# DeltaNet and top-2 experts on one core: the experts' part in a written order, and four early tiles instead of five

## The chip, the cores and the metric

One Trainium2 chip, one core. The metric is the device time of one execution in microseconds (us). The engines are named PE (TensorE), ACT (ScalarE), DVE (VectorE), POOL (GpSimd) and SP (SyncE, which here only issues DMAs). All data is fp32.

## The reference

A delta-rule attention over 4 batches, 8 heads, 768 steps and 48 columns a head; its output, as 3072 tokens of 384 columns, goes through a noisy top-2 router with 8 experts, each two matrices of 384 × 1024 and 1024 × 384 with a ReLU between.

```python
# attention, for each step t
y[:, :, t] = einsum('bhd,bhde->bhe', q[:, :, t], state)
v_old = einsum('bhde,bhd->bhe', state, kt)
state = state + bt * einsum('bhd,bhe->bhde', kt, vt - v_old)
# experts; x is y as (3072, 384)
noisy = x @ w_gate + log1p(exp(x @ w_noise)) * noise
# the two largest per token, their softmax is top2_w
for e in range(8):
    for k in range(2):
        mask = top2[:, k] == e
        out[mask] += top2_w[mask, k, None] * (relu(x[mask] @ w1[e]) @ w2[e])
```

## The kernel before

**Attention.** `deltanet()` computes attention in six steps of 128 positions (512 tokens each) and routes in four rounds: steps 0 and 1, 2 and 3, 4, 5. Every piece of it is a job for one engine, with a cost, what it reads and writes, and for some a due time; a planner (`Jobs`) writes out the order of all engines from these, and the program keeps to that order. As soon as a round is routed, each row of it (384 columns and four numbers: token, gates, expert) is spread by indirect DMAs (`spread`, L385) into `rows_x` in HBM, expert by expert: 3072 places for each expert, of which the first ones fill.

**Early tiles.** So that PE has work while the last steps are routed and spread, the first rows of expert 0 are computed inside this stage, in buffers that attention no longer needs (`early`, L1200). The table `EARLY` (L22) says which tiles of 128 rows: four tiles with tokens up to step 3 and a fifth one with tokens up to step 4. `cut` (L1165) moves the count of rows on, where fewer have come so far, so that these tiles hold only rows of the tokens so far. For a set of tiles, SP loads rows, PE transposes them (L1258), PE multiplies with `w1e` (L1284), ACT does the ReLU (L1294), PE multiplies with `w2e` (L1307), DVE multiplies with the gate (`early_gate`) on the way out of PSUM (L1321), and POOL scatters into `out_dram`, adding nothing yet (L426).

**Experts.** What follows is ordered by the scheduler of the framework, from the order in which the code stands and from its own estimates, so an instruction may pass others of its engine.

- `rest()` (L1666) does the remaining rows of expert 0 up to 832, here 192. SP loads them into `xq` (32 partitions, L1545) and their numbers into `m` (L1556); `places` (L1573) makes the index and the gate of each row on DVE (L1579, L401, L405); DVE turns `xq` into `xe_r` by 32 × 32 transposes (L1680); PE multiplies with `w1e` (L1688), ACT does the ReLU, PE multiplies with `w2e` (L1696 for the whole tile, L1701 for the last 64 rows); DVE multiplies with the gate (L1705 to L1707), POOL scatters. Between these, DVE makes the 21 sums of blocks of expert 1's `w1` (`add_up` with `SUMS_W`, L1502), POOL zeroes both `sums` (L1484) and makes the four sums of blocks of its `w2` (`t_w`, L1509), and the rows of expert 1 are loaded, turned into `xe` (L1588, six turns) and summed into `s_x` (`SUMS_X`, L1502, twelve sums).
- Experts 1 to 7 then have the same form, each with 832 rows. `first()` (L1593) computes the hidden layer by a fast block scheme: a table `PLAN` of 40 half products (two passes each, matmul at L1536 into one of five banks `inner`), with additions into `hT` on DVE (L1613), copies and ReLUs on ACT (L1619, L1608) and, on DVE, the sums of the hidden layer `s_h` (L1524), four for each half. `second()` (L1621) is a 2 × 2 scheme with seven products for each of three pairs of tiles; each product is followed by one or two additions into `sums` by DVE, times the gate (`add_gated`, L1438), and the steps share the banks `outer` and three of `inner`. The two first pairs go step by step together (`both`), then the third with the last 64 rows (`last_rows`, L1651).
- In the code, the preparation of the next expert stands in between: SP's loads at the start; the sums of `w1` on POOL and the next index and gate behind the hidden sums; two turns after each of three steps; all twelve row sums ahead of the third pair; after the last scatter (`put`) the sums of `w2` on POOL and the gathers (L417) that fetch what is in `out_dram` for the next expert's tokens into the other `sums`.
- At the end `values_load` reads the largest count of rows on all engines; only if an expert had more than 832 rows, a slow branch does the rest. It does not run here.

Of the kernel before, what the change touches and what calls it, by code (L numbers as in the profile page):

```python
# [9 lines left out]
FP32 = mybir.dt.float32  # L10
# [8 lines left out]
Q = 32  # L19
TILES = 6  # L20
MORE = 64
EARLY = {3: (0, 4), 4: (4, 5)}  # L22
# [207 lines left out]
def kernel(  # L230
# [201 lines left out]
    def deltanet(ictx):  # L432
# [754 lines left out]
        early_index, early_gate = sb([128, 5], "early_index", I32), sb([128, 5], "early_gate")  # L1187
# [12 lines left out]
        def early(s):  # L1200
# [12 lines left out]
            if lo == 0:  # L1213
                xr = old_k[0:4]
                xe = [*old_kT[0:2], old_q[0]]
                hT = old_k
                xr = [(x[:, 0:ROW], key) for x, key in xr]
                hT = [(x[:, 0:rows], key) for x, key in hT]
            else:
                (x, key), (y, key_y), *z = old_kT[2:6]  # L1220
                xr = [(x[:, 0:ROW], key)]
                xe = [(y[:, do * 128 : (do + 1) * 128], key_y) for do in range(KT)]
                hT = [
                    (z[fo // 4][0][:, fo % 4 * 128 : (fo % 4 + 1) * 128], z[fo // 4][1])
                    for fo in range(FT)
                ]
# [72 lines left out]
            for i in range(n):  # L1299
# [3 lines left out]
                for f0 in range(0, FT, 2):  # L1303
# [16 lines left out]
                    DVE, 0.6,  # L1320
                    lambda got=got, p=p, at=at: nc.vector.tensor_scalar_mul(  # L1321
# [125 lines left out]
    with ExitStack() as ectx:  # L1447
# [9 lines left out]
        bank_x = outer[0:2]  # L1457
# [13 lines left out]
        nc.tensor.matmul(bank_x[0][:, 0:E], ones, before)  # L1471
        nc.vector.tensor_copy(counts, bank_x[0][:, 0:E])
        nc.vector.tensor_reduce(out=most, in_=counts, axis=AX.X, op=ALU.max)
        nc.vector.tensor_copy(most_i, most)


# [6 lines left out]
        for got in sums:  # L1483
            nc.gpsimd.memset(got, 0.0)  # L1484

# [14 lines left out]
        def add_up(engine, sums, block):  # L1500
            for to, x, y, sign in sums:
                engine.tensor_tensor(  # L1502
                    out=block(to), in0=block(x), in1=block(y),
                    op=ALU.add if sign == "+" else ALU.subtract,
                )

# [159 lines left out]
        def rest():  # L1666

            w1e, w2e = w_even_tiles
            t0 = EARLY[4][1]
            rows = slice(t0 * 128, ROWS)  # L1670
            cols = rows.stop - rows.start
            got = sums[0]
            load_rows(
                0, rows.start,
                [(128, 0, rows.start, ROWS - MORE), (MORE, TILES - t0, ROWS - MORE, ROWS)],
            )
            index, gate = places(0, TILES - t0, TILES - t0)
            xe_r = moe.tile([128, KT, cols], FP32, name="xe_r")
            for b in range(KT):
                nc.vector.transpose(  # L1680
                    out=xe_r[:, b], in_=xq[:, rows.start // Q :, b:QD:KT]
                )
            load_rows(1)
            banks = [*inner, outer[2]]
            for fo in range(FT):
                p_h = banks[fo % 6][:, 0:cols]
# [5 lines left out]
                nc.scalar.activation(hT[:, fo, 0:cols], p_h, ACTF.Relu)  # L1692
            add_up(nc.vector, SUMS_W, blocks[0])
            p_o, p_m = bank_x[0][:, 0:DM], bank_x[1][:, 0:DM]
            for fo in range(FT):
                nc.tensor.matmul(  # L1696
                    p_o, hT[:, fo, 0:128], w2e[:, fo], start=(fo == 0), stop=(fo == FT - 1)
                )
            halves = [slice(lo, lo + MORE) for lo in (0, 64)]
            for fo in range(FT):  # L1700
                nc.tensor.matmul(  # L1701
                    p_m[halves[fo % 2]], hT[:, fo, 128:cols], w2e[:, fo],
# [185 lines left out]
```

## Time and profile before

| | |
|---|---|
| median of 3 runs | 863.03 us (862.18 to 864.03) |
| profiled execution | 860.22 us |
| its span, first to last instruction | 858.1 us |
| mean granted clock of PE over the span | 0.896 of full speed |
| experts 1 to 7, start of the first product (us) | 424.27, 487.11, 550.35, 610.00, 669.66, 729.35, 788.72 |
| end of PE's last pass | 847.39 us |

Times in the trace count from the first instruction. A row of the timeline is a group of equal instructions that follow each other: its start, the time from the start of the first to the end of the last, engine, line, operation, output and inputs, shapes and count. In brackets stands the idle time ahead of it on its engine and what ended that. Instructions of an engine overlap a little, so n of them take less than n times the duration of one. A matmul of fp32 data is recorded as two passes.

### The profile page before, as it was taken

How to read it: one execution, taken by the hardware profiler on the slowest of the kernel's cores; microseconds unless marked ns; L12 is line 12 of the kernel's file. 1: busy time of each engine (PE TensorE's matmuls, PEld its weight loads, DVE VectorE, ACT ScalarE, POOL GpSimd, SP SyncE). 2: the span in 40 equal slices, each digit the busy share in tenths (PEclk: the TensorE clock that was granted, in tenths of full speed). 3: DMA queues.
4: the chain of work that ended last, by engine and by line, in shares of the span. 5: the costliest groups of instructions: out<-in, count | busy, mean ns of one | idle time of the engine just before them, and what ended most of it. 6: DMA issues, size and time to landing. Idle time of an engine off the chain costs nothing.

```text
span 858.1 us, 21611 instructions
## 1 busy us (share of the span) xinstructions
PE 749.2 (87%) x8957; PEld 576.1 (67%) x8957; DVE 591.0 (69%) x1347; ACT 310.4 (36%) x733; POOL 389.8 (45%) x424
## 2 busy tenths in 40 slices
PE   4756879887898898993899999999999999999995
PEld 3546668776697785562548748759668678587594
DVE  5996899989978653007479589388487595694651
ACT  3573558755734543110152141150240330520510
POOL 3021312121552745116275774576684785776311
PEclk8566959895769799996999999999999999999998
DMA  4789733724522323601664626317325425401201
GB/s 65 135 231 258 154 95 99 196 55 131 132 80 58 118 88 125 208 25 36 141 164 108 156 59 144 121 56 167 123 96 103 140 82 99 145 0 58 58 25 37
DMA packets 141724, 93.74 MB, mean 109 GB/s; under 512 B 115242, under 2 KB 134089, under 8 KB 140592
## 3 DMA queue, kind: packets, MB, share of 16 engines
q1 hardware_dynamic: 129952, 64.54, 31.3%
q0 software_dynamic: 9552, 27.33, 9.5%
q8 instruction: 72, 1.18, 0.5%
q10 hardware_dynamic: 2112, 0.39, 0.3%
q14 instruction: 36, 0.29, 0.1%
HBM read 58.82 MB, written 34.81 MB: 109 GB/s over the span
## 4 chain that ended last, share of the span: by engine, by line
PE 52%; DVE 14%; issue 3%; ACT 1%; POOL 0%; DVEq 0%; POOLq 0%; ACTq 0%
PE inner L1536 22%; PE outer L1536 11%; DVE s_x L1502 4%; PE pair L1284 3%; PE pair L1307 3%; PE inner L1659 2%; DVE sums L1438 2%; DVE s_h L1524 2%; DVE xe L1588 2%; PE single L860 1%; PE single L936 1%; DVE hT L1613 1%; PE pair L569 1%; PE inner L1688 1%; PE single L925 1%
## 5 line engine op out<-in xcount | busy, mean ns | idle before, releaser
L1619 ACT ACTIVATE hT<-inner 128x416 f32<-128x416 f32 x105 | 54.0, 515 | 247.0 <-PE inner L1536 246.0
L1613 DVE TENSOR_TENSOR hT<-hT,inner 128x416 f32<-128x416 f32 x182 | 102.6, 581 | 39.8 <-PE inner L1536 26.9
L426 POOL DMA_INDIRECT out_dram<-sums,index x51 | 53.9, 1058 | 106.2 <-DVE sums L1438 86.4
L1536 PE MATMUL inner<-s_x,w1e 128*128 128x416 f32 x196 | 80.5, 522 | 0.4 <-DVE s_x L1502 0.4
L1438 DVE SCALAR_TENSOR_TENSOR sums<-outer,gate,sums 128x192 f32<-128x192 f32 (+1 forms) x113 | 45.6, 413 | 50.9 <-PE outer L1536 50.8
L1608 ACT ACTIVATE hT<-hT 128x416 f32<-128x416 f32 x112 | 61.0, 549 | 47.0 <-DVE hT L1613 42.7
L903 POOL COPY wide<-st 64x384 f32<-64x384 f32 x44 | 25.0, 569 | 104.5 <-DVE st L890 82.9
L417 POOL DMA_INDIRECT sums<-out_dram,index x49 | 56.0, 1143 | 35.9 <-issue 27.6
L697 DVE TENSOR_TENSOR t<-t,part 128x30 f32<-128x30 f32 (+9 forms) x180 | 64.9, 360 | 6.2
L693 DVE TENSOR_TENSOR part<-t 128x30 f32<-128x30 f32 (+9 forms) x180 | 61.6, 342 | 5.0
L1536 PE MATMUL outer<-t_w,hT 128*128 128x192 f32 x336 | 59.5, 327 | 4.9 <-DVE sums L1438 4.9
L1536 PE MATMUL inner<-xe,w1e 128*128 128x416 f32 x140 | 59.8, 526 | 3.8 <-DVE xe L1588 3.8
L1536 PEld LDWEIGHTS inner<-s_x,w1e 128*128 128x128 f32 x196 | 36.6, 191 | 35.3 <-issue 25.7
L385 POOL DMA_INDIRECT rows_x<-y,slot x48 | 47.0, 978 | 28.7 <-DVE early_gate L405 9.2
L1536 PEld LDWEIGHTS outer<-t_w,hT 128*128 128x128 f32 x336 | 55.0, 190 | 6.5 <-issue 6.5
L1536 PE MATMUL inner<-s_x,s_w 128*128 128x416 f32 x140 | 59.1, 519 | 0.0
L1502 POOL TENSOR_TENSOR w1e<-w1e 128x256 f32<-128x256 f32 x54 | 49.2, 922 | 7.1 <-DMA w1e<-in_moe_w_dram 6.1
L1536 PE MATMUL outer<-w2e,hT 128*128 128x192 f32 x280 | 50.1, 326 | 0.0
L1536 PEld LDWEIGHTS outer<-w2e,hT 128*128 128x128 f32 x280 | 46.5, 190 | 2.4 <-issue 2.4
L662 POOL TENSOR_SCALAR_AFFINE_SELECT t<-t 128x1024 f32<-128x1024 f32 x6 | 7.6, 1268 | 85.8 <-DVE ss L633 73.4
L860 PE MATMUL single<-v,w 64*64 64x48 f32 x768 | 35.9, 258 | 10.3 <-ACT w L788 3.8
L1536 PEld LDWEIGHTS inner<-xe,w1e 128*128 128x128 f32 x140 | 26.8, 196 | 25.7 <-issue 18.3
(214 smaller groups left out, 1642.1 us busy)
## 6 DMA issues: line engine op xcount, KB each, us to landing
w1e<-in_moe_w_dram SPq DMA_DIRECT2D x8, 1536.0 KB
w2e<-in_moe_w_dram SPq DMA_DIRECT2D x8, 1536.0 KB
xq<-rows_x SPq DMA_DIRECT2D x28, 312.0 KB
rows_x<-empty SPq DMA_DIRECT2D x8, 776.0 KB
qp<-in_q_dram SPq DMA_DIRECT2D x48, 96.0 KB
v<-in_v_dram SPq DMA_DIRECT2D x48, 96.0 KB
out_dram<-empty SPq DMA_DIRECT2D x4, 1152.0 KB
kp<-in_k_dram SPq DMA_DIRECT2D x44, 96.0 KB
```

Source lines behind the costliest of these rows:

```text
L385: d = nc.gpsimd.indirect_dma_start(out=rows_x, out_offset=bass.IndirectOffsetOnAxis(ap=slot, axis=0), in_=rows, in_offset=None,).ins
L417: nc.gpsimd.indirect_dma_start(out=got, out_offset=None, in_=out, in_offset=bass.IndirectOffsetOnAxis(ap=index, axis=0), bounds_check=N - ...
L426: nc.gpsimd.indirect_dma_start(out=out, out_offset=bass.IndirectOffsetOnAxis(ap=index, axis=0), in_=got, in_offset=None, bounds_check=N - ...
L693: v_.tensor_tensor(out=part, in0=t[:, :, j + 1 :, j, None].to_broadcast(shape), in1=t[:, :, None, j, 0:j].to_broadcast(shape), op=ALU.mult,)
L697: v_.tensor_tensor(out=t[:, :, j + 1 :, 0:j], in0=t[:, :, j + 1 :, 0:j], in1=part, op=ALU.add)
L860: nc.tensor.matmul(per_head(p_u)[b, h], w64[b, h], v_n[b, h], start=(h == 0), stop=(h == H - 1), skip_group_check=True,)
L1438: nc.vector.scalar_tensor_tensor(out=got, in0=p, scalar=gate, in1=got, op0=ALU.mult, op1=ALU.add)
L1502: engine.tensor_tensor(out=block(to), in0=block(x), in1=block(y), op=ALU.add if sign == "+" else ALU.subtract,)
L1536: nc.tensor.matmul(p, lhsT, rhs, start=opens and i == 0, stop=i == len(products) - 1, skip_group_check=True,)
L1608: nc.scalar.activation(h, h, ACTF.Relu)
L1613: nc.vector.tensor_tensor(out=h, in0=h, in1=p, op=ALU.add if sign > 0 else ALU.subtract)
L1619: nc.scalar.mul(h, p, float(sign))
```

## The change

- `EARLY` is `{3: (0, 4)}`: the fifth early tile and its `cut` go, and `rest()` computes 320 rows of expert 0 (two tiles of 128 and one of 64) in its place.
- The gating of the early tiles (`got`) moves from DVE to ACT.
- The experts' part stands in a function `experts()` that runs under `tc.manual_schedule()`: every engine does its instructions in the order in which the code writes them.
- The order at its start is new: expert 0's last rows, their transposes and gates, expert 1's rows, sums of `w2` and zeroing on POOL, sums of `w1`, turns, places and row sums on DVE, all of it ahead of `rest()`; then the counts and the gathers.
- In an expert, one turn and the next places come behind the first four half steps of the two first pairs; of the other turns and the row sums two stand behind each further step of these (`fill(2)`), one behind each step of the third pair, three behind the last rows. The scatter of the last rows comes sooner. The sums of `w2` come after all scatters.
- The largest count is read on all engines after expert 1.

```diff
-EARLY = {3: (0, 4), 4: (4, 5)}
+EARLY = {3: (0, 4)}
...
                 jobs.add(
-                    DVE, 0.6,
-                    lambda got=got, p=p, at=at: nc.vector.tensor_scalar_mul(
+                    ACT, 0.6,
+                    lambda got=got, p=p, at=at: nc.scalar.mul(
                         got[:, 0:DM], p.tile[:, 0, 0:DM], early_gate[:, at : at + 1]
                     ),
...
+        def experts():
+            w_even_tiles, weights = held_weights, load_weights(w_odd, 1)
+            first_weights = w_even_tiles
+            blocks = blocks_of(*weights)
+            load_rows(
+                0, rest0,
+                [(128, 0, rest0, ROWS - MORE), (MORE, TILES - t0, ROWS - MORE, ROWS)],
+            )
+            xe_r = moe.tile([128, KT, cols], FP32, name="xe_r")
+            for b in range(KT):
+                nc.vector.transpose(
+                    out=xe_r[:, b], in_=xq[:, rest0 // Q :, b:QD:KT]
+                )
+            index, gate = places(0, TILES - t0, TILES - t0)
+            load_rows(1)
+            sums_of_second(blocks[1])
+            for got in sums:
+                nc.gpsimd.memset(got, 0.0)
             add_up(nc.vector, SUMS_W, blocks[0])
+            for x in TURNS:
+                turn(*x)
+            next_index, next_gate = places(1, TILES, TILES)
+            for emit in add_up_later(SUMS_X, xb):
+                emit()
+            added = rest(first_weights, xe_r, index, gate, sums[0])
...
+                first(a1, iter(of_hidden[0]))
+                for emit in of_hidden[1]:
+                    emit()
+                between = iter(())
+                if follows:
+                    add_up(nc.gpsimd, SUMS_W, blocks[0])
+                    between = iter(
+                        [lambda x=x: turn(*x) for x in TURNS] + add_up_later(SUMS_X, xb)
+                    )
...
+                for part in (0, 1):
+                    both(1, part)
+                    both(2, part)
+                fill(1)
+                if follows:
+                    next_index, next_gate = places(e + 1, TILES, TILES)
+                for n in (5, 6, 3, 7, 4):
+                    both(n)
+                    fill(2)
+                for i in (0, 1, 3, 4):
+                    put(i)
+                for n in (5, 1):
+                    pairs[2][n - 1]()
+                    fill(1)
+                last_rows(w2e, gate, got)
+                fill(3)
+                put(TILES)
+                for n in (6, 3, 7, 2, 4):
+                    pairs[2][n - 1]()
+                    fill(1)
+                put(2)
+                put(5)
+                if follows:
+                    sums_of_second(blocks[1])
...
+                if e == 1:
+                    count = nc.values_load(most_i[0:1, 0:1], min_val=0, max_val=N)
...
+        with tc.manual_schedule():
+            added, count = experts()
```

The order of the instructions on the engines at three places shows what moved. The first is DVE between the last piece of the routing (`before`, L1016, in the change L1017) and the transposes of expert 0's last rows. The rows of before:

```order
L1016 TENSOR_TENSOR before<-before,r_count 128x8
L1321 TENSOR_SCALAR qp_139<-pair_111,early_gate 128x384
...
L1472 COPY counts<-outer_5486 128x8
L1473 TENSOR_REDUCE most<-counts 128x1
L1474 CAST most_i<-most 128x1
L1502 TENSOR_TENSOR w1e<-w1e 128x256 x2
...
L1502 TENSOR_TENSOR w1e<-w1e 128x256 x4
L1680 STREAM_TRANSPOSE xe_r<-xq 128x192 x2
```

And those of the change:

```order
L1017 TENSOR_TENSOR before<-before,r_count 128x8
L1706 STREAM_TRANSPOSE xe_r<-xq 128x320 x3
L1568 CAST index_5480<-m_5440 128x2
...
L1482 TENSOR_TENSOR w1e<-w1e 128x256 x4
L1577 STREAM_TRANSPOSE xe<-xq 128x416 x6
L1568 CAST index_5528<-m_5441 128x6
...
L1489 TENSOR_TENSOR s_x_5456<-xe 128x416
```

In before, five early multiplications, each of which needs a finished bank of PE, the counts and all 21 sums of `w1` stand ahead of `xe_r`; in the change nothing does, and the turns and row sums of expert 1 follow without anything of `rest()` between.

The second place is DVE in the second product of an expert, from the last hidden sum on. Before:

```order
L1524 TENSOR_TENSOR s_h_5494<-hT,s_h_5493 128x2x384
L1438 SCALAR_TENSOR_TENSOR sums_5496<-outer_5486,gate_6160,sums_5496 128x192
...
L1438 SCALAR_TENSOR_TENSOR sums_5496<-inner_5482,gate_6160,sums_5496 128x192
L1588 STREAM_TRANSPOSE xe<-xq 128x416
L1438 SCALAR_TENSOR_TENSOR sums_5496<-inner_5484,gate_6160,sums_5496 128x192
L1502 TENSOR_TENSOR s_x_5518<-xe 128x416
L1502 TENSOR_TENSOR s_x_5519<-xe 128x416
L1438 SCALAR_TENSOR_TENSOR sums_5496<-inner_5481,gate_6160,sums_5496 128x192
```

The change:

```order
L1513 TENSOR_TENSOR s_h_5436<-hT,s_h_5435 128x2x384
...
L1428 SCALAR_TENSOR_TENSOR sums_5437<-inner_5424,gate_5800,sums_5437 128x192
L1577 STREAM_TRANSPOSE xe<-xq 128x416
L1568 CAST index_6136<-m_5441 128x6
L402 SCALAR_TENSOR_TENSOR gate_6137<-m_5441 128x6
L406 TENSOR_TENSOR gate_6137<-gate_6137,m_5441 128x6
...
L1428 SCALAR_TENSOR_TENSOR sums_5437<-inner_5426,gate_5800,sums_5437 128x192
L1428 SCALAR_TENSOR_TENSOR sums_5437<-inner_5423,gate_5800,sums_5437 128x192
L1577 STREAM_TRANSPOSE xe<-xq 128x416 x2
```

In before, five of the six turns stand among the additions of the first product and the row sums `s_x` begin here; in the change all six turns and the six operations on the next places stand here, and all but one of the row sums stand behind the fourth of these steps.

The third place is POOL at the end of an expert. Before, the sums of `w2` (L1509) stand between the last scatters:

```order
L426 DMA out_dram<-sums_5495,index_5822 3072x384 x4
L1509 TENSOR_TENSOR t_w_5514<-w2e 128x768
L1509 TENSOR_TENSOR t_w_5515<-w2e,t_w_5514 128x768
L426 DMA out_dram<-sums_5495,index_5822 3072x384
L1509 TENSOR_TENSOR t_w_5516<-w2e 128x768
```

In the change they stand behind all seven, ahead of the gathers:

```order
L427 DMA out_dram<-sums_5438,index_5528 3072x384 x7
L1498 TENSOR_TENSOR t_w_5452<-w2e 128x768
L1498 TENSOR_TENSOR t_w_5453<-w2e,t_w_5452 128x768
L1498 TENSOR_TENSOR t_w_5454<-w2e 128x768
L1498 TENSOR_TENSOR t_w_5455<-w2e,t_w_5453 128x768
L418 DMA sums_5437<-out_dram,index_5799 128x384 x6
```

So the order of the four sums themselves is the same, and the last scatters no longer wait for them.

## Rows read from the trace of the kernel before

**Rows 1.** The page, busy time (us), share and instructions of each engine, whole span.

```profile
PE 749.2 (87%) x8957; PEld 576.1 (67%) x8957; DVE 591.0 (69%) x1347; ACT 310.4 (36%) x733; POOL 389.8 (45%) x424
```

**Rows 2.** Stretches: length, each engine's busy us (instructions), PEclk, DMA share, GB/s.

```profile
388.20:402.00 13.80, 0.39 (x2) 0.30 (x2) 13.18 (x27) 0.00 (x0) 12.91 (x7) 0.67 0.04 13
424.30:487.10 62.80, 60.98 (x264) 43.55 (x265) 50.16 (x98) 16.09 (x31) 43.23 (x38) 0.98 0.54 125
550.35:610.00 59.65, 58.75 (x265) 43.24 (x265) 42.17 (x76) 15.97 (x31) 40.15 (x39) 1.00 0.43 115
```

**Rows 3.** What PE waited for from 330 us on: us in total, times, longest.

```profile
PE inner L1688 <- DVE xe_r L1680: 12.9, 1, 12.9
PE outer L1536 <- DVE sums L1438: 4.9, 6, 1.4
PE inner L1536 <- DVE xe L1588: 3.8, 1, 3.8
```

**Rows 4.** Timeline of PE, start, us, engine, line, operation [idle before <- releaser].

```profile
355.71 20.80 PE L1307 MATMUL pair<-w2e,kp 128*128 128x384 f32 x64
376.35 0.50 PE L1258 MATMUL pair<-ident,kT 128*128 128x128 f32 x3
...
402.11 7.52 PE L1688 MATMUL inner<-xe_r,w1e 128*128 128x192 f32 x30 [12.93 <-DVE xe_r L1680]
...
417.64 2.80 PE L1701 MATMUL outer<-w2e,hT 128*64 128x384 f32 x16
424.27 1.06 PE L1536 MATMUL inner<-xe,w1e 128*128 128x416 f32 x1 [3.83 <-DVE xe L1588]
```

**Rows 5.** Timeline of DVE in the same stretch.

```profile
389.68 0.75 DVE L1502 TENSOR_TENSOR w1e<-w1e 128x256 f32<-128x256 f32 x2
...
395.38 6.24 DVE L1502 TENSOR_TENSOR w1e<-w1e 128x256 f32<-128x256 f32 x4
401.54 0.73 DVE L1680 STREAM_TRANSPOSE xe_r<-xq 128x192 f32<-128x192 f32 x2
...
421.67 3.78 DVE L1588 STREAM_TRANSPOSE xe<-xq 128x416 f32<-128x416 f32 x6
```

**Rows 6.** Timeline of SP's DMA issues, loads of `xq` for expert 0 and 1.

```profile
349.12 4.26 SPq L1545 DMA_DIRECT2D xq<-rows_x  x4
...
403.68 2.50 SPq L1545 DMA_DIRECT2D xq<-rows_x  x4
```

**Rows 7.** Timeline of PE, first and last passes of expert 7.

```profile
788.72 1.56 PE L1536 MATMUL inner<-xe,w1e 128*128 128x416 f32 x4
...
845.93 1.46 PE L1536 MATMUL outer<-t_w,hT 128*128 128x192 f32 x8
```

**Rows 8.** Timeline of expert 3's second product, PE and DVE.

```profile
583.83 2.76 PE L1536 MATMUL inner<-t_w,s_h 128*128 128x192 f32 x16
585.01 1.05 DVE L1438 SCALAR_TENSOR_TENSOR sums<-outer,gate,sums 128x192 f32<-128x192 f32 x3
...
595.08 0.57 DVE L1502 TENSOR_TENSOR s_x<-s_x,xe 128x416 f32<-128x416 f32 x1
...
595.30 2.84 PE L1536 MATMUL outer<-t_w,hT 128*128 128x192 f32 x16 [0.90 <-DVE sums L1438]
```

**Rows 9.** Timeline of DVE, one gate operation with POOL quiet and beside its sums.

```profile
404.33 0.16 DVE L401 SCALAR_TENSOR_TENSOR gate<-m 128x6 f32<-128x6 f32 x1
...
510.19 0.72 DVE L401 SCALAR_TENSOR_TENSOR gate<-m 128x6 f32<-128x6 f32 x1
```

**Rows 10.** Timeline of POOL, expert 3: last gather, last weights' sums.

```profile
565.76 0.95 POOL L417 DMA_INDIRECT sums<-out_dram,index  x1 [0.30 <-issue]
...
582.84 4.89 POOL L1502 TENSOR_TENSOR w1e<-w1e 128x256 f32<-128x256 f32 x5
```

**Rows 11.** Timeline of PE ahead of the early tiles.

```profile
333.05 0.41 PE L1065 MATMUL single<-r_taken,mask_u 128*128 128x32 f32 x2 [1.89 <-DVE r_taken L1016]
...
337.00 2.56 PE L1284 MATMUL pair<-kT,w1e 128*128 128x512 f32 x4
```

More of the change, by code (lines that the diff above doesn't have):

```diff
@@ L1212, in early @@
             old_q = [(flat(qps(i)), halves("q", i % NQ)) for i in range(NQ)]
[L1213 to L1226, printed above, removed]
+            xe = [*old_kT[0:2], old_q[0]]
+            xr = [(x[:, 0:ROW], key) for x, key in old_k[0:4]]
+            hT = [(x[:, 0:rows], key) for x, key in old_k]
             def load_rows(i):
@@ L1505, in add_up, with add_up_later @@
                 )
+        def add_up_later(sums, block):
+            return [
+                lambda to=to, x=x, y=y, sign=sign: nc.vector.tensor_tensor(
+                    out=block(to), in0=block(x), in1=block(y),
+                    op=ALU.add if sign == "+" else ALU.subtract,
+                )
+                for to, x, y, sign in sums
+            ]
         def sums_of_second(b2):
@@ L1664, in last_rows, with rest @@
                 add_gated(got[0:MORE, TILES], p[half], gate[0:MORE, TILES : TILES + 1])
[L1666 to L1684, printed above, removed]
+        t0 = EARLY[3][1]
+        rest0, cols = t0 * 128, ROWS - t0 * 128
+        def rest(weights, xe_r, index, gate, got):
+            w1e, w2e = weights
+            tiles = rows_in[t0:]
             for fo in range(FT):
-                p_h = banks[fo % 6][:, 0:cols]
+                p_h = inner[fo % 5][:, 0:cols]
                 for do in range(KT):
@@ new lines, in rest @@
+            added = []
+            for i, size in enumerate(tiles):
+                p = outer[i][:, 0:DM]
+                halves = [slice(lo, lo + MORE) for lo in (0, 64)]
+                for fo in range(FT):
+                    lhsT = hT[:, fo, i * 128 : i * 128 + size]
+                    if size == 128:
+                        nc.tensor.matmul(
+                            p, lhsT, w2e[:, fo], start=(fo == 0), stop=(fo == FT - 1)
+                        )
+                    else:
+                        nc.tensor.matmul(
+                            p[halves[fo % 2]], lhsT, w2e[:, fo], start=(fo < 2),
+                            stop=(fo >= FT - 2), skip_group_check=True,
+                        )
+                g = gate[0:size, i : i + 1]
+                if size == 128:
+                    nc.vector.tensor_scalar_mul(got[:, i], p, g)
+                else:
+                    nc.vector.tensor_scalar_mul(got[0:size, i], p[halves[0]], g)
+                    add_gated(got[0:size, i], p[halves[1]], g)
+                added.append(
+                    scatter(got[0:size, i], index[0:size, i : i + 1], "out0", first_out)
+                )
@@ L1799 @@
+        held_weights, first_out = weights, added
+        with tc.manual_schedule():
+            added, count = experts()
     place = const.tile([128, NT], FP32, name="place")
```

157 lines of the change are left out of this document (55 added, 102 removed).

## The prediction

> **What bounds the kernel now.** I read the busy times first, then the experts' part cut into stretches, then the list of what TensorE waited for, and last the timelines round the two places where it waited longest. Over the whole span TensorE (PE) is busy 87% and VectorE (DVE) 69% [rows 1], an average over stages of different kinds. The stretches separate them [rows 2]: between 388.2 and 402.0 us PE works 0.39 of 13.80 us, while an ordinary expert (550.35 to 610.00) keeps it busy 58.75 of 59.65. So there is one hole ahead of the experts and a small loss in each. The list of waits names what ends them [rows 3]: 12.9 us, once, for the transposes `xe_r` of expert 0's last rows; 3.8 us, once, for the transposes `xe` of expert 1's rows; 4.9 us in six pieces for DVE's additions into `sums`.
>
> The timelines say why. PE ends the four-tile second product near 376.35 and begins the fifth early tile; the product of expert 0's rest starts at 402.11 after an idle 12.93 us, directly after the first transposes of `xe_r` at 401.54 [rows 4, 5]. Their rows were asked for at 349.12 [rows 6], so they had been there for long: DVE's own queue held them, with the weights' sums ahead, the last four of which took 6.24 us at 395.38 [rows 5]. The same happens once more: expert 1's rows were asked for only at 403.68 [rows 6], since `xq` had to be emptied by those transposes first, and the six turns stand behind the gating of expert 0's rest: 421.67, 3.78 us long, and PE goes on at 424.27 [rows 4, 5].
>
> **The change, part by part.** The sum is made on the profiled execution, 860.22 us, which is 2.81 us below the median of the runs, 863.03; I add that back at the end.
>
> *Start of the experts, PE's work.* One early tile goes and expert 0's rest grows from 192 to 320 rows. Each fp32 product stands as two passes in the trace. A 384-column pass costs 20.80/64 = 0.325 us [rows 4], so one of 320 columns about 0.325 × 320/384 = 0.271. First product: 8 × 3 products, 48 passes, 13.0 us. Second product: 16 passes for each of two whole tiles, 32 × 0.325 = 10.4 us, and 2.8 us for the 64 rows, as in the trace [rows 4]. With 0.4 for the hand-over between stages that is 26.6 us. It takes the place of the 47.9 us from 376.35 to 424.27 [rows 4]. Besides, two 512-column passes move ahead of the router's counting, into the 1.89 us in which PE waited there [rows 11]: 2 × 0.325 × 512/384 = 0.9 us. Start of expert 1: 376.35 + 26.6 − 0.9 = 402.1 instead of 424.27, **22.2 us** sooner.
>
> *What has to be ready for that.* DVE has nothing left between the router's last count and `xe_r`, since the early gating goes to ScalarE. The rows load at 349.12 and must be turned by 376; even 10 us for the transfer and 2 for the three transposes leave over 10 us. Then come 21 weight sums, 8 us at 0.75 for two [rows 5]; the load of expert 1's rows lands meanwhile; six turns (3.8 us [rows 5]) and twelve row sums at 0.57 [rows 8], 6 to 7 us. With rows there at 355 that ends near 375 to 385, and it is wanted at 402. This slack of some 20 us is the cover of every DVE step I cost at nothing here. If it were gone, the turns would be late next. POOL's zeroing of `sums` moves behind its second-product sums and is wanted when PE has the first whole tile, near 393: both start after the fourth early scatter, near 377, where POOL has nothing else. ScalarE takes four multiplications of one 128 × 384 tile each, 5.2 us of PE apart: nothing, even at 1 us apiece. The load of `most_i` on every queue moves from the end to between experts 1 and 2: from nothing to 0.5 us, I take 0.3.
>
> *The experts.* From 424.27 to PE's end at 845.93 + 1.46 = 847.39 are 423.1 us [rows 4, 7]. The last expert has no next rows to prepare and runs without holes: 847.39 − 788.72 = 58.67 us [rows 7]. Seven of them would be 410.7, so 12.4 us is all that the rest of the change can give back: expert 1 lasts 62.8 us, and an ordinary one 59.65 [rows 2]. What is left in an ordinary one is the wait at 595.30, 0.90 us [rows 8]. PE starts the steps with hidden sums at 583.83, and after four of them, at 594.4, it wants a bank for which DVE must first have done eleven additions into `sums`; from 585.01 on DVE did these, a turn and eleven row sums. The written order puts six turns, the six operations on next places and one row sum there instead, and the other eleven sums among the third pair's steps and the last rows, where each step takes 1.3 us of PE and at most about 1.2 of DVE. In DVE's time: 11 × 0.33 (1.05 us for three, overlapping [rows 8]) = 3.6; six turns 3.8 [rows 5] to 4.4; a row sum 0.5; and the places. These cost 0.16 us for the larger gate operation when POOL is quiet and 0.72 when POOL is adding weights [rows 9]: 0.7 us for the six at best, 2.8 at worst. The hidden sums should be done a good 1 us sooner than 585.01, since no turn stands among the first product's additions any more. So DVE is ready 8.6 to 11.3 us after about 583.9, at 592.5 to 595.2, and PE asks at 594.4: a wait of 0 to 0.8 us. I take 0.4 for each of six experts, 2.4 us in all. The experts then give 12.4 − 2.4 − 0.3 = **9.7 us**.
>
> *A rule that speaks against this.* The gate operation's 0.72 us beside POOL's additions, against 0.16 [rows 9], is a DVE instruction waiting for POOL's. The Trainium skill, page "SBUF — State Buffer", section "Who interferes with whom", says that a DVE instruction with two SBUF inputs and a GpSimd instruction that reads SBUF take turns at a shared port pair for a whole instruction, so that one fully blocks the other; the trace agrees with it here. By that rule all four gate operations, now written behind the first additions, would wait a whole POOL instruction each in every expert, which is the 2.8 us; by the quiet row the six cost 0.7 and no wait is left. The sum would be 833.5 by the one (0.8 us a time) and 828.7 by the other; further along the same road lies the second rival.
>
> *POOL's queue.* All seven scatters now stand ahead of the four second-product sums, and the gathers and weights' sums behind them. In the trace the last gather starts at 565.76 and the weights' sums end at 587.73 [rows 10], 37.4 us into the expert; they are wanted at about 59. A few us later costs nothing.
>
> **Sum:** 22.2 + 9.7 = 31.9; 860.22 − 31.9 = 828.3; on the median 863.03 − 31.9 = **831.1**.
>
> **The rivals.**
> 1. *More goes.* DVE keeps up fully, so the 2.4, the 0.3 and the 0.4 fall away: 828.0; and the passes after PE's early wait, four of which took 2.56 us [rows 11] where four at 0.433 take 1.7, run at full speed, 1 to 2 us: 826. For it: every term above has cover. Against: the price of the places. Chance 0.13.
> 2. *DVE stays the bound in the second product.* The places cost 2.8 us, the hidden sums wait for POOL as they do now, and 0.9 to 1.4 us remain in each expert: 3 to 6 us less gain, 834 to 837. For it: DVE has as much to do ahead of that step as before. Chance 0.2.
> 3. *The hole closes only in part.* The rows and the weights land late, or one instruction written early holds DVE until 390: 8 to 14 us of the 22 remain: 839 to 845. Against: the rows were asked for at 349.12. Chance 0.06.
> 4. *Slower.* The written order delays POOL: gathers and weights' sums run after everything else, and if the sums end later than 59 us into an expert each next first product waits for them. It is 37.4 now, so they would have to slip 21 us before it costs anything, and by a further 31.9/6 = 5.3 us in each expert to eat the gain; at 7 us of waiting an expert the time would be 873. Nothing moved on POOL is that long. Chance 0.02.
> 5. *No effect*, because another late input (the load of the weights) holds PE at the old place: 863. Chance 0.02.
>
> **How the numbers follow.** My forecast (829 to 833.5) has 0.57, and its number is **831.0**. The range leaves out rivals 4 and 5 and most of 3 above, and reaches into rival 1 below: **826 to 840**. A measurement of this kernel can tell about 0.2%, 1.7 us, from no change; the cases give faster 0.96, same 0.02, slower 0.02.
>
> **What would show it.** In the profile after: no wait of PE for `xe_r` or `xe`; expert 0's rest starting at about 376 and expert 1 near 402; granted clock at full speed there, where 388.2 to 402.0 showed 0.67 [rows 2]; `xe_r` turned before 360 and the row sums done before 390; experts of 59.1 us each, expert 1 included. Wrong would be: `xe_r` behind anything on DVE; experts still at 59.6 with waits for `sums` (rival 2); PE waiting for POOL's sums `s_w` or `w1e` (rival 4).

## The result, and the profile after

The change took 832.22 us (median of 4 runs, 830.2 to 833.09) against 862.61 of the kernel before (4 runs, 855.25 to 864.03): a ratio of 0.966, 95% interval 0.960 to 0.972. The profiled execution went from 860.22 to 832.40 us, and the trace divides these 27.8 us as follows.

| stretch (us) | before | after | gain | forecast |
|---|---|---|---|---|
| start to the early tiles' second product | 355.71 | 353.99 | 1.7 | 0.9 |
| from there to expert 1 | 68.56 | 46.95 | 21.6 | 21.3 |
| experts 1 to 7 on PE | 423.12 | 419.94 | 3.2 | 9.7 |
| PE's end to the end of the execution | 12.83 | 11.52 | 1.3 | 0 |

What PE waited for from 330 us on (us in total, times, longest) shows the two ends at once. The waits for `xe_r` and `xe` of [rows 3] are gone; the one for `sums` has grown from 4.9 us in six pieces to 7.9 in seventeen, in two lines, since some now fall on a bank of `inner`:

```profile
PE outer L1525 <- DVE sums L1428: 6.2, 12, 0.6
PE inner L1525 <- DVE sums L1428: 1.7, 5, 0.3
```

The timeline of PE in the stretch of [rows 4] has no bracket left: the rest follows the early tiles, and expert 1 the rest, without a wait.

```profile
353.99 20.80 PE L1297 MATMUL pair<-w2e,kp 128*128 128x384 f32 x64
374.63 13.08 PE L1665 MATMUL inner<-xe_r,w1e 128*128 128x320 f32 x48
387.55 10.48 PE L1677 MATMUL outer<-w2e,hT 128*128 128x384 f32 x32
397.97 2.80 PE L1681 MATMUL outer<-w2e,hT 128*64 128x384 f32 x16
...
400.94 1.64 PE L1525 MATMUL inner<-xe,w1e 128*128 128x416 f32 x4
```

On DVE, where [rows 5] had the transposes at 401.54 and the turns at 421.67, they now come at 353.00 and 364.06, as soon as their rows have landed (the brackets), and the last row sums end at 375.2, when PE has only just begun the rest:

```profile
353.00 1.61 DVE L1706 STREAM_TRANSPOSE xe_r<-xq 128x320 f32<-128x320 f32 x3 [16.11 <-DMA xq<-rows_x]
...
361.84 1.67 DVE L1482 TENSOR_TENSOR w1e<-w1e 128x256 f32<-128x256 f32 x4
364.06 3.87 DVE L1577 STREAM_TRANSPOSE xe<-xq 128x416 f32<-128x416 f32 x6 [0.55 <-DMA xq<-rows_x]
...
374.10 1.09 DVE L1489 TENSOR_TENSOR s_x<-s_x,xe 128x416 f32<-128x416 f32 x2
```

The last four sums of `w1` take 1.67 us here, where they took 6.24 [rows 5]. There they stood beside POOL's sums of `w2` (394.55 to 403.29); in the change these begin only at 376.73 (in e10, too, the four take 1.68 us ahead of POOL's). So some 4.6 us of the old wait of 12.93 come from this neighbour, and not from the length of DVE's queue.

Stretches of the change, columns as in [rows 2]: the rest, expert 1, an ordinary expert and the last one. The granted clock is 1.00, its higher level of 2.4 GHz, where 388.20 to 402.00 had 0.67; expert 1 has lost its extra 2 us; but the ordinary expert takes 60.28 us, 0.6 more than before:

```profile
374.63:400.94 26.31, 26.31 (x99) 16.34 (x98) 1.91 (x5) 4.08 (x9) 14.70 (x9) 1.00 0.32 93
400.94:461.56 60.62, 59.25 (x267) 43.48 (x267) 47.83 (x86) 16.08 (x31) 32.34 (x35) 1.00 0.40 109
521.88:582.16 60.28, 58.93 (x265) 43.43 (x265) 46.37 (x82) 16.09 (x31) 40.61 (x40) 1.00 0.43 114
762.55:820.88 58.33, 58.33 (x266) 43.41 (x264) 32.41 (x58) 16.09 (x31) 21.71 (x19) 1.00 0.14 44
```

Where those go is seen in expert 3, with the timeline of DVE and PE, beside [rows 8]. The hidden sums take 1.3 to 1.5 us each and end 34.2 us into the expert; three of the four operations on the gates (L402, L406) take 0.63 to 0.73 us each; PE then waits three times:

```profile
550.51 1.46 DVE L1513 TENSOR_TENSOR s_h<-hT 128x768 f32<-128x768 f32 x1
...
554.70 1.48 DVE L1513 TENSOR_TENSOR s_h<-hT,s_h 128x768 f32<-128x768 f32 x1
...
556.10 1.05 DVE L1428 SCALAR_TENSOR_TENSOR sums<-outer,gate,sums 128x192 f32<-128x192 f32 x3
...
558.11 0.73 DVE L402 SCALAR_TENSOR_TENSOR gate<-m 128x6 f32<-128x6 f32 x1
...
560.24 0.72 DVE L1428 SCALAR_TENSOR_TENSOR sums<-inner,gate,sums 128x192 f32<-128x192 f32 x2
...
560.70 2.87 PE L1525 MATMUL inner<-w2e,s_h 128*128 128x192 f32 x16 [0.32 <-DVE sums L1428]
...
566.55 2.84 PE L1525 MATMUL outer<-t_w,hT 128*128 128x192 f32 x16 [0.38 <-DVE sums L1428]
...
574.76 1.26 DVE L1428 SCALAR_TENSOR_TENSOR sums<-inner,gate,sums 64x384 f32<-64x384 f32 x2 [1.82 <-PE inner L1648]
...
577.69 0.42 DVE L1428 SCALAR_TENSOR_TENSOR sums<-outer,gate,sums 128x192 f32<-128x192 f32 x1
...
578.16 1.57 PE L1525 MATMUL outer<-t_w,hT 128*128 128x192 f32 x8 [0.65 <-DVE sums L1428]
```

### The profile page after: what moved, and what is told of

It reads as the page before. It is cut to its first block, busy times and chain, and to the rows that moved or that the text cites. A ratio compares the mean times of both kernels' runs of the same rounds, so it can differ in the third digit from the quotient of the medians.

```text
span 830.6 us, 21554 instructions
## 1 busy us (share of the span) xinstructions
PE 739.9 (89%) x8904; PEld 569.4 (69%) x8904; DVE 603.6 (73%) x1338; ACT 310.8 (37%) x726; POOL 385.3 (46%) x424
## 4 chain that ended last, share of the span: by engine, by line
PE 44%; DVE 15%; issue 8%; POOL 3%; ACT 1%; DVEq 0%; POOLq 0%; ACTq 0%
PE inner L1525 20%; PE outer L1525 7%; DVE sums L1428 3%; DVE s_h L1513 3%; DVE xe L1577 3%; PE pair L1297 2%; PE pair L1274 2%; PE inner L1648 2%; DVE s_x L1489 2%; PE inner L1665 2%; PE outer L1677 1%; PE single L861 1%; PE pair L570 1%; PE single L937 1%; POOL out_dram L427 1%
## 5 line engine op out<-in xcount | busy, mean ns | idle before, releaser
L1602 DVE TENSOR_TENSOR hT<-hT,inner 128x416 f32<-128x416 f32 x182 | 105.1, 586 | 45.3 <-PE inner L1525 36.1
L427 POOL DMA_INDIRECT out_dram<-sums,index x52 | 52.2, 1005 | 127.9 <-DVE sums L1428 109.3
L418 POOL DMA_INDIRECT sums<-out_dram,index x49 | 51.8, 1056 | 19.2 <-issue 11.1
L1525 PE MATMUL inner<-s_x,s_w 128*128 128x416 f32 x140 | 56.9, 513 | 0.0
L1525 PE MATMUL inner<-xe,w1e 128*128 128x416 f32 x140 | 55.8, 513 | 0.0
L1482 POOL TENSOR_TENSOR w1e<-w1e 128x256 f32<-128x256 f32 x54 | 51.4, 961 | 2.0
L1525 PEld LDWEIGHTS inner<-s_x,s_w 128*128 128x128 f32 x140 | 26.6, 190 | 22.2 <-issue 22.1
```

The source lines that it names most:

```text
L418: nc.gpsimd.indirect_dma_start(out=got, out_offset=None, in_=out, in_offset=bass.IndirectOffsetOnAxis(ap=index, axis=0), bounds_check=N - ...
L427: nc.gpsimd.indirect_dma_start(out=out, out_offset=bass.IndirectOffsetOnAxis(ap=index, axis=0), in_=got, in_offset=None, bounds_check=N - ...
L1482: engine.tensor_tensor(out=block(to), in0=block(x), in1=block(y), op=ALU.add if sign == "+" else ALU.subtract,)
L1525: nc.tensor.matmul(p, lhsT, rhs, start=opens and i == 0, stop=i == len(products) - 1, skip_group_check=True,)
L1602: nc.vector.tensor_tensor(out=h, in0=h, in1=p, op=ALU.add if sign > 0 else ALU.subtract)
```

## The experiments

Totals of these runs can't be set beside those of the change: the kernel before took 868.05 us beside some of them and 888 to 899 beside others. The difference lies ahead of the early tiles' second product, which begins between 354 and 392 us. When the change was run again (`after_again`), this mark came 32.0 us later than in its first trace, with a granted clock of 0.72 between 200 and 300 us and of 0.80 from there to the mark (0.77 and 0.95 in the first), and the total was 31.9 us longer. From the mark to expert 1 the traces of equal code agree to 0.1 us: 46.95 us in the change, when it was run again, and in every kernel that keeps its start. So stretches are compared, not totals, and the totals named in the expectations were missed for this reason: by 2 to 5 us in e1, e2, e5 and e6, by 28 in `after_again`. Two questions were open: which part of the change closed the hole ahead of the experts, and what is left in an expert.

### What closed the hole

**The scheduler's order, all else as in the change** (`e6_no_written_order`).

```diff
-        with tc.manual_schedule():
-            added, count = experts()
+        added, count = experts()
```

> The code of the change, but the experts' part is ordered by the scheduler again (the written order taken away, everything else kept: four early tiles, gating on ACT, the counts after the rest). DVE then has the 21 sums of w1 ahead of the transposes of expert 0's rows again, and the six turns behind the gating of the rest. Theory S (the hole ahead of the experts closed because the early gating and the count left DVE's queue, so that the sums of w1 run beside the early tiles): no wait of PE for the first transposes, the rest starts near 375 us; only the turns stay late, PE waits 3 to 4 us for them, and expert 1 starts at 404 to 405 us in place of 400.9; experts as before, 59.7 us; the run 838 to 840. Rival W (the written order itself closed the hole): PE waits 10 us or more for the transposes of the rest, expert 1 starts after 410, the run above 845.

Theory S held: 51.05 us from the mark to expert 1, no wait for the transposes of the rest, and one of 3.95 us for the turns, which the scheduler again puts behind the gating of the rest. Experts 1 to 7 took 423.1 us, as before. PE in this kernel:

```profile
356.66 20.80 PE L1297 MATMUL pair<-w2e,kp 128*128 128x384 f32 x64
377.30 13.08 PE L1665 MATMUL inner<-xe_r,w1e 128*128 128x320 f32 x48
...
407.71 3.14 PE L1525 MATMUL inner<-xe,w1e 128*128 128x416 f32 x4 [3.95 <-DVE xe L1577]
```

**The gating on ACT, alone** (`e7_before_act`): the kernel before with one edit.

```diff
-                    DVE, 0.6,
-                    lambda got=got, p=p, at=at: nc.vector.tensor_scalar_mul(
+                    ACT, 0.6,
+                    lambda got=got, p=p, at=at: nc.scalar.mul(
```

> The kernel before with one edit: the gating of the early tiles on ACT. Theory S (the hole needs the early gating and the count of rows both out of DVE's queue): the count still stands ahead of the sums of w1 on DVE and still waits for PE's end of the fifth tile, so the hole stays: 67 to 68.5 us from the start of the early second product to expert 1, against 68.56 before. Rival G (the gating's engine alone closed it): 52 to 56 us.

455.45 − 386.85 = 68.60 us, against 68.56: nothing. PE waits as long as before, since the count of rows still stands ahead of the sums of `w1` on DVE and still needs PE's last early tile (DVE idles 39.44 us until 420.41, and the last four sums take 6.24 us beside POOL's again):

```profile
386.85 20.80 PE L1307 MATMUL pair<-w2e,kp 128*128 128x384 f32 x64
...
419.99 0.39 PE L1471 MATMUL outer<-before,ones 128*128 128x8 f32 x2 [0.67 <-ACT qp L1321]
433.31 7.49 PE L1688 MATMUL inner<-xe_r,w1e 128*128 128x192 f32 x30 [12.93 <-DVE xe_r L1680]
...
455.45 3.05 PE L1536 MATMUL inner<-xe,w1e 128*128 128x416 f32 x4 [3.83 <-DVE xe L1588]
```

**The gating on ACT, and the count behind the rest** (`e10_count_late_act`), in the kernel before:

```diff
-        nc.tensor.matmul(bank_x[0][:, 0:E], ones, before)
-        nc.vector.tensor_copy(counts, bank_x[0][:, 0:E])
...
         added = rest()
+        nc.tensor.matmul(bank_x[0][:, 0:E], ones, before)
+        nc.vector.tensor_copy(counts, bank_x[0][:, 0:E])
...
```

> The kernel before with two edits: the early gating on ACT, and the count of rows behind the rest of expert 0; five early tiles and the scheduler's order as before. Theory S: the sums of w1 and the transposes of the rest run on DVE beside the fifth tile, PE goes from that tile straight into the rest, and only the six turns stay late: 32.4 + 15.8 + 4 = about 52 us from the early second product to expert 1; experts as before. Rival W (it takes the written order): 60 us or more.

435.83 − 383.41 = 52.42 us: 16.1 of the 21.6 us come from these two edits, with five tiles and the scheduler. PE goes from the fifth tile straight into the rest at 415.71, and what stays is the wait for the turns:

```profile
383.41 20.80 PE L1307 MATMUL pair<-w2e,kp 128*128 128x384 f32 x64
...
415.71 5.04 PE L1684 MATMUL inner<-xe_r,w1e 128*128 128x192 f32 x30
...
435.83 1.75 PE L1532 MATMUL inner<-xe,w1e 128*128 128x416 f32 x2 [3.95 <-DVE xe L1584]
```

**Five early tiles, all else as in the change** (`e8_five_early`: `EARLY` and the branch of `early` for the fifth tile put back).

```diff
-EARLY = {3: (0, 4)}
+EARLY = {3: (0, 4), 4: (4, 5)}
```

> Five early tiles and 192 rows of the rest as in the kernel before, all else as in the change. PE's work from the early second product to expert 1 is then 20.8 + 11.8 for the fifth tile + 7.8 + 5.2 + 2.8 = 48.4 us and a few tenths of hand-over. Theory S (the written order and the gating on ACT are enough; the fifth tile costs its extra passes and its own stages alone): expert 1 starts 48.5 to 50 us after the start of the early second product, against 46.95 in the change. Rival F (the fifth tile holds DVE and the transposes of the rest up, as in the kernel before): 55 us or more.

439.95 − 391.62 = 48.33 us, a little under the expected range: leaving the fifth tile out is worth 1.4 us, and no wait for DVE comes with it:

```profile
391.62 20.80 PE L1308 MATMUL pair<-w2e,kp 128*128 128x384 f32 x64
...
439.95 1.64 PE L1536 MATMUL inner<-xe,w1e 128*128 128x416 f32 x4
```

**The gating of the four early tiles back on DVE, all else as in the change** (`e4_gating_dve`; the edit of e7 turned round).

> The gating of the four early tiles back on DVE, all else as in the change. In the written order the transposes of expert 0's rows then stand behind the fourth multiplication, which waits for PE's last early tile. Theory S: PE waits some 2.5 us for the transposes (the multiplication 0.6, the transposes 1.6, signals), the rest starts 23.1 us after the early second product does in place of 20.64; DVE's chain behind it (sums of w1, turns, places, row sums, some 19 us) ends about when the rest's first product and first tiles do, so expert 1 starts 2.5 us later, 49.5 us after that mark in place of 46.95. Rival N (the multiplication's engine is of no account): 46.95 as before. Rival L (DVE's chain ends too late): more than 51 us.

50.10 us, 3.15 more than the change where 2.5 were expected: 1.31 for the transposes, which I had put at 2.5, and a second wait of 1.53 that I had priced at nothing. DVE begins its chain at 411.08 and comes to the rest's gating only at 438.89, 27.8 us later, and the count waits for a bank that this gating must empty. The 19 us that I had named are there, from 419.62 on. Ahead of them stand the transposes, 1.6 us, and the six operations on the rest's places: these take 7.0 us (412.58 to 419.62) beside POOL's sums of `w2` (412.43 to 419.68), where they take 0.6 in the change. DVE, then PE:

```profile
412.58 1.72 DVE L1568 CAST index<-m 128x2 int32<-128x2 f32 x1
...
419.62 0.74 DVE L1482 TENSOR_TENSOR w1e<-w1e 128x256 f32<-128x256 f32 x2
```

```profile
389.70 20.80 PE L1297 MATMUL pair<-w2e,kp 128*128 128x384 f32 x64
411.81 13.16 PE L1665 MATMUL inner<-xe_r,w1e 128*128 128x320 f32 x48 [1.31 <-DVE xe_r L1706]
...
439.55 0.39 PE L1721 MATMUL outer<-before,ones 128*128 128x8 f32 x2 [1.53 <-DVE sums L1687]
```

**The written order alone** (`e11_order_alone`: five tiles and the gating on DVE, else the change).

> The written order alone: five early tiles and the early gating on DVE as in the kernel before, else the change. The transposes of the rest then stand behind the fifth multiplication: PE waits about 2 us for them, the rest starts 34 to 35 us after the early second product. Behind them DVE has 8 us of sums of w1, 4 of turns, 1 of places and 6 of row sums ahead of the rest's gating, some 19 us, against 16 us of PE: the count's bank waits for that gating, and expert 1 starts 52 to 54 us after the mark. Rival (the rest's work on PE hides all of it): 50 to 51 us; rival (the hole comes back): 60 or more.

449.70 − 388.26 = 61.44 us, where I expected 52 to 54. The number is that of the second rival, but the old hole did not come back: PE waits 1.14 us for the transposes, and the loss is the second wait of e4, now 11.56 us. DVE's chain starts behind the fifth multiplication at 420.66 and lasts until 448.59, 27.9 us. I had taken it at 19 us behind the transposes; but its start now runs beside POOL's sums of `w2`, which come behind the last early scatter, and the tiny operations on the rest's places take as long as these, 5.8 us for the six (422.18 to 427.99). DVE, then POOL, then PE:

```profile
420.66 0.62 DVE L1322 TENSOR_SCALAR qp<-pair,early_gate 128x384 f32<-128x384 f32 x1 [10.94 <-PE pair L1308]
...
422.21 2.20 DVE L402 SCALAR_TENSOR_TENSOR gate<-m 128x1 f32<-128x1 f32 x1
...
424.58 1.71 DVE L402 SCALAR_TENSOR_TENSOR gate<-m 64x1 f32<-64x1 f32 x1
...
448.59 0.61 DVE L1698 TENSOR_SCALAR sums<-outer,gate 128x384 f32<-128x384 f32 x1
```

```profile
422.54 1.83 POOL L1509 TENSOR_TENSOR t_w<-w2e 128x768 f32<-128x768 f32 x1
```

```profile
449.25 0.60 PE L1732 MATMUL outer<-before,ones 128*128 128x8 f32 x2 [11.56 <-DVE sums L1698]
449.70 3.12 PE L1536 MATMUL inner<-xe,w1e 128*128 128x416 f32 x4
```

A gate operation of 64 × 1 elements took 1.71 us beside sums of 1.8 us each, against 0.14 in the change (at 354.90); there these operations are over before POOL begins its sums. The Trainium skill, page "SBUF — State Buffer", section "Who interferes with whom", says that a DVE instruction with two SBUF inputs and a GpSimd instruction that reads SBUF block each other for a whole instruction, and the trace agrees: a gate operation takes 0.7 us beside POOL's sums of `w1` (0.73 each) and 1.7 to 2.2 beside those of `w2` (1.8 each). Not every one of them waits (0.15 at 414.21 in e4), and some with a single input do: the conversion at 412.58 there took 1.72.

Together, in us from the mark to expert 1:

| early tiles | gating | count | order | us |
|---|---|---|---|---|
| 5 | DVE | ahead of the rest | scheduler (before) | 68.56 |
| 5 | ACT | ahead | scheduler | 68.60 |
| 5 | ACT | behind | scheduler | 52.42 |
| 4 | ACT | behind | scheduler | 51.05 |
| 5 | ACT | behind | written | 48.33 |
| 4 | ACT | behind | written (the change) | 46.95 |
| 4 | DVE | behind | written | 50.10 |
| 5 | DVE | behind | written | 61.44 |

With the gating on ACT and the count behind the rest, the other two parts simply add: 1.4 us for four tiles under either order, 4.1 for the written order with either number of tiles (e10 and e6 differ also in the order in which the code stands). Under the written order the gating on ACT is worth 3.2 us with four tiles and 13.1 with five. The count behind the rest without the gating on ACT, in the scheduler's order, was not tried.

### What is left in an expert

**Row sums ahead of the last rows' additions** (`e1_fill`).

```diff
-                last_rows(w2e, gate, got)
                 fill(3)
+                last_rows(w2e, gate, got)
```

> The three row sums that stand behind the additions of the last 64 rows stand ahead of them, on DVE alone. In the changed kernel DVE is idle for 1.82 us there, and PE then waits 0.65 us for `sums` two steps later (the third wait of each expert). Theory A (the loss that is left in an expert, 60.3 us against 58.3 for the last one, is DVE's written order at three places): this third wait goes in all six experts, with the slow start behind it 0.8 to 0.9 us each, and an expert takes 59.4 us, the run about 827. Rival C (DVE has too much to do in the second product as a whole, so a wait only moves): a wait of about the same length turns up in one of the steps behind, and an expert stays at 60.0 to 60.3 us.

The third wait is gone from all six experts, and they take 58.84 to 59.62 us in place of 59.76 to 60.62: 0.9 to 1.0 less in experts 1, 5 and 6, as expected, and 1.4 to 1.5 less in 2 to 4, where the first wait is gone as well. That can't be put down to this edit: the first wait is missing in one expert of the change too (expert 5, which takes 59.76 us), and in another when it was run again (expert 3). No wait took its place; rival C fell.

**The places to the end of the expert** (`e2_places`).

```diff
                 fill(1)
-                if follows:
-                    next_index, next_gate = places(e + 1, TILES, TILES)
...
                 for n in (6, 3, 7, 2, 4):
                     pairs[2][n - 1]()
                     fill(1)
+                    if n == 2 and follows:
+                        next_index, next_gate = places(e + 1, TILES, TILES)
```

> The six operations on the next expert's places move on DVE from behind the first four additions into `sums` to behind the sixth step of the third pair, where POOL makes no sums. Theory A: the first two waits of each expert (0.34 and 0.40 us, with the slow starts behind them 1.2 us) go, the third stays at 0.65; the six operations take about 0.7 us in all in place of 2.3; an expert takes 59.1 us, the run about 825.5. Rival C: the waits move to later steps and an expert stays above 60 us. Rival D (the index is late for the gathers, which then delay POOL's sums): a wait of PE for POOL in the next expert's first product.

The first two waits are gone from all six, the third stays at 0.65, and an expert takes 59.07 us (expert 1: 59.32). The same larger gate operation is quick at its new place:

```profile
580.42 0.16 DVE L402 SCALAR_TENSOR_TENSOR gate<-m 128x6 f32<-128x6 f32 x1
```

**No sums on POOL** (`e5_no_pool_sums`). It leaves out the 21 sums of `w1` for experts 2 to 7, so PE multiplies with old ones; the work on PE and DVE is otherwise the same.

```diff
-                    add_up(nc.gpsimd, SUMS_W, blocks[0])
```

> Leaves out the 21 sums of blocks of w1 on POOL for experts 2 to 7; all else stands as in the change. Theory B (the first two waits of each expert are POOL's reads that hold up DVE's hidden sums and gate operations): the hidden sums take 0.95 us each in place of 1.3 to 1.5, the larger gate operation 0.16 in place of 0.73, DVE reaches the additions of the hidden-sum steps some 3 us sooner, the first two waits go and the third (0.65) stays: an expert takes 59.1 us, the run about 825.5. Rival (the number of DVE instructions there is too large whatever they last): the first two waits stay at 0.2 us or more each and an expert stays near 60.

Theory B held: 59.07 us (expert 1: 59.16), the first two waits gone, the third as before. DVE does the same instructions in the same order; only their times differ, 0.95 for a hidden sum and 0.17 for the gate operation:

```profile
551.32 0.95 DVE L1513 TENSOR_TENSOR s_h<-hT 128x768 f32<-128x768 f32 x1
...
557.04 0.17 DVE L402 SCALAR_TENSOR_TENSOR gate<-m 128x6 f32<-128x6 f32 x1
...
561.02 2.76 PE L1525 MATMUL inner<-w2e,s_h 128*128 128x192 f32 x16
...
577.75 1.57 PE L1525 MATMUL outer<-t_w,hT 128*128 128x192 f32 x8 [0.64 <-DVE sums L1428]
```

**Both moves** (`e3_both`), with the change beside it on the same chip (`after_again`).

> The change once more, beside the next kernel on the same chip. From the start of the early tiles' second product to expert 1 it should take 46.95 us as in every run with this start so far, and an ordinary expert 60.3 us; 830 to 836 us, as the attention ahead of it varies by some us from run to run.

> Both moves together: the three row sums ahead of the last rows' additions, and the places behind the sixth step of the third pair. Theory A: none of the three waits is left, an ordinary expert takes 58.4 to 58.6 us (the last one, without next rows, takes 58.3), six of them 10 to 11 us less than in the change, which the run should be faster than by 10 us. Rival C (the two savings overlap, or DVE is late elsewhere once the waits are gone): 58.9 us or more in an expert, 8 us or less.

Medians of 6 runs: 851.27 us for both moves and 864.26 for the change; against the kernel before 0.954 (0.950 to 0.959) and 0.967 (0.963 to 0.972). The intervals lie apart: this version is faster than both kernels, and 13 us faster than the change, where 10 were expected. Its experts take 407.5 us in place of 420.1. In its trace PE waits for nothing from the early tiles' second product to its end, and an expert with next rows takes no longer than the last one (58.32), which has none (expert 1 and expert 3; columns as in [rows 2]):

```profile
438.17:496.53 58.36, 58.36 (x267) 43.53 (x266) 46.44 (x86) 16.09 (x31) 32.26 (x35) 1.00 0.41 113
554.69:612.85 58.16, 58.16 (x266) 43.49 (x265) 45.11 (x82) 16.09 (x31) 40.56 (x40) 1.00 0.43 118
```

## Why the prediction was right, and where it was not

The forecast was 831.0 us with a range of 826 to 840, and 832.22 was measured. Its terms are less good than its sum: start and end together gave 24.6 us (1.7 + 21.6 + 1.3) where 22.2 stood, and the experts 3.2 where 9.7 stood. That the number came within 1.2 us is in part luck: the profiled executions differ by 27.8 us where 31.9 stood, and the medians by 30.4. The 0.2% that a measurement was said to tell apart was too little as well: the kernel before ranged from 855.25 to 864.03 us.

**The start was right by its steps.** PE's work from 376.35 on was put at 26.6 us and took 26.3 (374.63 to 400.94): 13.08, 10.48 and 2.80 for the three products, 13.0, 10.4 and 2.8 in the sum. All that was to be ready was: `xe_r` turned by 354.6, the row sums done by 375.2, POOL's zeroing over before the first gating. The 0.9 us for two passes moved into PE's early wait can't be told apart: the mark came 1.7 us sooner in this execution, but in kernels with the same start it lies between 354 and 391 us, and between 356.7 and 359.8 on one chip alone (e1, e2, e5). What I did not see is that the part of the change that looks smallest, the count of rows placed behind the rest, is needed for most of it: without it the gating on ACT gave nothing (e7), with it 16.1 us (e10).

**The experts failed by their size.** The sum had 0.4 us of waiting left in each; there were 1.4 us in three waits, and 2.0 with the slow passes that follow one (58.33 to about 60.3). The one wait that the sum had priced, at the bank that PE wants after four steps, came out as it stood there: 0.38 at 566.55, with 10.3 us from 556.10 to the end of the eleventh addition, inside the 8.6 to 11.3. The other two it had put at nothing: 0.32 us two steps sooner (560.70) and 0.65 behind the last rows (578.16). Three terms were wrong.

- "where each step takes 1.3 us of PE and at most about 1.2 of DVE": not behind the last rows. There DVE has two additions (1.26 us for both) and three row sums ahead of the next step's addition, 2.9 us, which PE wants after two steps of 1.3. The rows show it: the last rows' additions at 574.76, the next addition at 577.69, PE's wait of 0.65 at 578.16. Just ahead of those additions DVE had been idle for 1.82 us; e1 put the sums there.
- "The hidden sums should be done a good 1 us sooner": they were done 34.2 us into the expert, against 34.7 (585.01 − 550.35). They begin 0.9 us sooner without turns among the additions of the first product, but all four are now held up by POOL's sums beside them (1.3 to 1.5 us each, 0.95 without these in e5). In before POOL's sums stood beside them too, but the first two kept 0.93 and 0.92 us, and the sums beside those took 1.48 and 1.53. Besides, POOL's sums of `w1` now last until 563.3, 41.4 us into the expert where it was 37.4 [rows 10], and so lie beside all of the places. The traces point to their own order: the change has done three of the 21 when POOL goes on after its last wait for PE, 25.4 us into the expert, and before had done nine at the same point (25.7 us). The prediction said of POOL's queue that "A few us later costs nothing"; this holds for PE, which waits for none of these sums, and not for DVE beside them. POOL in the change, and in before:

```profile
547.33 1.53 POOL L1482 TENSOR_TENSOR s_w<-w1e,s_w 128x256 f32<-128x256 f32 x2 [3.22 <-PE inner L1525]
```

```profile
576.09 1.55 POOL L1502 TENSOR_TENSOR s_w<-w1e,s_w 128x256 f32<-128x256 f32 x2 [0.90 <-PE inner L1536]
```

- The places took 2.2 us, inside the 0.7 to 2.8 that I allowed; but they stand ahead of an addition that PE wants after two steps already, and there no wait was priced. Moving them away takes both of the first waits out (e2).

So rival 2, with a chance of 0.2, had the mechanism of the first two waits, which cost 1.2 us in an ordinary expert (60.28 to 59.07 in e2 and e5). The third, 0.9 us (e1), stood in no rival. The total still fell by 3.2 us because expert 1 and 2 had lost far more before (62.84 and 63.24 us, now 60.62 and 60.32) than the four others lose now (0.1 to 0.9 us each). The rule that I set against the forecast, by which the sum was 833.5, was right about the places: e5 shows that the first two waits go without its mechanism (and e2 that they go without the places there), and that it has no part in the third, which stays at 0.64.

**The tail.** The 1.3 us at the end were not forecast, and their cause stays open. The kernels with the old code of the experts (before, e7, e10) need 12.4 to 12.8 us from PE's end to the end, those with the new code 11.3 to 12.2, though e5 needs 13.1. The load of `most_i`, which left the end, is not what counts: in e6 PE, DVE and POOL still load it at the end (POOL at 831.34, PE's last pass ends at 830.84), and e6 needs 11.6. What differs in the traces is a pause on POOL ahead of its last drain, 0.9 to 1.0 us in before, e7 and e10 and at most 0.05 in all others.

## What to carry to other kernels

An instruction that waits for a far engine holds everything behind it on its own, and taking one such instruction out shows nothing while a second stands behind it: list all of them before pricing one. When an order is written by hand, cut the engine's queue at each bank that another engine wants next and add up what stands between, at the durations beside the neighbours that it will really have. What is moved on POOL has to be priced twice, by who waits for it and by which DVE instructions come to lie beside it: here two additions out of PSUM kept their time beside POOL's sums (0.72 us at 560.24, 0.69 at 564.10 without them), while a gate operation took up to 2.2 us in place of 0.15.

## What was not expected of the hardware

- A wait of PE costs more than its length: 0.32 us ahead of the sixteen passes at 560.70 came with 2.87 us for the sixteen where 2.76 is usual, and the passes began 0.49 us late (the two steps ahead lie 2.60 us apart, from 555.01 to 557.61).
- The multiplication by the gate of a 128 × 384 tile out of PSUM takes 0.58 us on ACT and 0.62 on DVE, so that here it can be placed by queue alone:

```profile
359.35 0.58 ACT L1311 ACTIVATE qp<-pair,early_gate 128x384 f32<-128x384 f32 x1 [4.51 <-PE pair L1297]
```
